# A decode block on one core: wo in contiguous blocks, the last K load ahead of the last V loads, the MLP weights in pieces

## The chip, the cores and the metric

The kernel runs on one core of a Trainium2 chip. The metric is the device time of one execution in microseconds (us). The profiled execution has a *span*, from its first to its last instruction; the timed number is about 1.8 us longer. Here a run counts as slow when it is over 1.5% above the fastest of its kernel.

## The reference

One token for each of four sequences goes through an attention block with a K/V cache and then an MLP. The shapes decide everything: the cache is 268 MB, the weights are 15 MB, the arithmetic is tiny.

```python
# x: (4,1,640) bf16; k_cache, v_cache: (4,32,4096,128); wq: (640,4096); wo: (4096,640)
# w1: (640,1728); b1: (1728); w2: (1728,640)
def A(x):                                     # attention
    q = (x @ wq).reshape(4, 1, 32, 128).transpose(0, 2, 1, 3)
    p = softmax(einsum("bhqd,bhkd->bhqk", q, k_cache) * 128 ** -0.5)
    return einsum("bhqk,bhkd->bhqd", p, v_cache).transpose(0, 2, 1, 3).reshape(4, 1, 4096) @ wo
def B(x):                                     # MLP with mish
    h = x @ w1 + b1
    return (h * tanh(softplus(h))) @ w2
h = x + A(layernorm(x))
return h + B(layernorm(h))
```

## The kernel before

The cache is read in 64 *tiles*. A tile is two heads of one sequence: 2,048 KB of K and 2,048 KB of V, each one load in which a partition takes one run of 16,384 bytes (64 positions of 128 numbers). I write K62 for the K load of tile 62; the last one is 63. All large loads come from one queue, in the order of the program, and the trace has 16 completions of each, which I take for one of each of the core's 16 DMA engines.

```python
LA = 3                                        # loads are issued three tiles ahead
stream = ctx.enter_context(tc.tile_pool(name="stream", bufs=8))     # 8 slots of 2 MB
def load_wo():                                # runs of 1,280 bytes, into three of the K/V slots
    for h0 in range(0, H, WOH):
        ...
        nc.sync.dma_start(
            out=v, in_=A_wo[h0 * Dh : (h0 + nh) * Dh, :].rearrange("(h p) n -> p h n", p=P))
...
WO_AT = NT - 4                                # wo is loaded ahead of tile 60, the MLP weights last
for i in range(NT + 1):
    if i + LA < NT:
        if i + LA == WO_AT:
            load_wo()
        load_kv(i + LA)                       # K, then V
    elif i + LA == NT:
        load_mlp()
    ...
```

Each tile passes through four steps. VectorE (DVE) multiplies K by q, in two halves (`prod`). TensorE (PE) sums the products with an identity as weights into PSUM (where the kernel keeps the sums of its matmuls), 256 columns at a time (`red`, called the fold below), DVE adds up what is left (`s_f`), ScalarE (ACT) takes exp (`e`). Then PE multiplies with V: 64 matmuls a tile, each with 128x128 of V as weights and two columns of e.

```python
def emit_pv(i):
    ...
    for r in range(R):                        # R = 64
        nc.tensor.matmul(o_ps[hg][:, b, :], lhsT=vt[i][:, r, :], rhs=e_bufs[i % NE][:, r, :],
                         start=(r == 0), stop=(r == R - 1))
```

After the last tile all products with wo follow in the tail (`y_ps`), then the layernorm and the MLP (`h_ps`, `act`, `y2_ps`).

The softmax here doesn't subtract the row's maximum and nothing guards it: scores larger than these inputs give would overflow.

## Time and profile before

| | before |
|---|---|
| time, median of 3 runs | 693.4 us |
| profiled span | 691.6 us |
| bytes moved | 283.4 MB |
| K62 landed | 650.6 us |
| K63 landed | 660.3 us |
| last load (end of w2) landed | 677.2 us |

From the page of the kernel before: the span; busy time, share of the span and number of instructions by engine; the rate in 40 slices of 17.3 us; packet sizes; one of the DMA queues; and the chain that ended last.

```profile
span 691.6 us, 14314 instructions
...
PE 486.5 (70%) x6663; PEld 383.4 (55%) x6663; DVE 338.4 (49%) x263; ACT 64.6 (9%) x288; POOL 1.6 (0%) x14
...
GB/s 373 428 424 428 431 422 425 430 425 428 425 428 427 425 426 429 425 424 431 425 425 427 427 426 427 424 429 426 424 427 430 424 427 426 417 337 427 420 373 18
DMA packets 25815, 284.28 MB, mean 411 GB/s; under 512 B 2260, under 2 KB 8092, under 8 KB 8732
...
q8 instruction: 52, 0.85, 0.5%
...
DMA 76%; PE 15%; DVE 7%; issue 1%; SPq 0%; DVEq 0%; ACT 0%
```

The stream runs at 424 to 430 GB/s nearly all the time; no compute engine is full. It is short of that in the first slice, in the slice around 610 us (337 GB/s) and in the last two. The line "q8 instruction" is the one that matters most later, and I passed over it: 52 packets, 0.85 MB, so 16 KB each, are fetches of instructions, and the page counts their time on the same 16 DMA engines as that of the data (0.5% of their span). PE has 6,663 matmuls and as many weight loads, so 13,326/52 = 256 instructions to a fetch; in the kernel after it is 11,792/46 = 256 and in e9 6,514/25 = 261.

The windows view of the kernel before (each line: start:end, length, busy time of the engines, then PE clock, DMA share and GB/s at the end) shows what the two weak places cost.

```profile
0.00:600.00 600.00, 430.39 (x5707) 336.90 (x5708) 304.71 (x222) 55.73 (x254) 1.56 (x14) 0.77 1.00 425
600.00:624.00 24.00, 14.25 (x200) 11.37 (x198) 7.59 (x5) 1.97 (x9) 0.00 (x0) 0.74 0.96 352
624.00:670.00 46.00, 29.27 (x405) 23.42 (x405) 20.89 (x15) 2.77 (x16) 0.00 (x0) 0.69 1.01 421
670.00:677.00 7.00, 5.40 (x190) 5.27 (x187) 0.71 (x2) 1.98 (x5) 0.00 (x0) 0.72 0.55 196
```

From 600 to 624 us the rate is 352 GB/s: at 427 this loses 24 x (1 - 352/427) = 4.2 us. There wo comes in small packets (1,280 bytes, 0.059 us each on average, 22 GB/s per engine; a packet of 16,384 bytes took 0.616 us, 26.6 GB/s), and its last part waits for a slot (4.7 us for PE's `o_ps` in the issue that stands from 610.16 to 615.47 us; the rate from 608 to 610 us is 224 GB/s). From 670 to 677 us the rate is below half.

The chain that ended last, from the kernel before (start, length, what). Its end:

```profile
646.33 14.02 DMA k_6961<-in_A_k_cache_dram
...
660.47 2.30 DVE prod L225
...
672.04 2.10 PE y_ps L297 x76
...
675.90 1.78 issue
...
678.45 0.42 PE y_ps L297 x10
...
680.14 2.09 PE h_ps L361 x70
```

K63 lands at 660.35, its multiply starts at 660.47, and the last product with wo is done at 678.87. From there to the end there are 12.7 us of layernorm and MLP, among them the 70 small matmuls of the first MLP product:

```profile
L361 PE MATMUL h_ps<-hb,w_sb x70: 166/167/215, 679.9 to 682.0; 128*128 128x5 bf16 x65, 128*64 128x5 bf16 x5
```

### The profile page before, as it was taken

The page shows a single profiled execution, that of the slowest core. Times are in us where ns is not written, and L with a number is a line of the kernel's source. Part 1 is how long each engine was busy: PE and PEld are TensorE (multiplying, and loading weights), DVE is VectorE, ACT ScalarE, POOL GpSimd, SP SyncE. Part 2 cuts the span into 40 slices and gives each one's busy share as a digit, 9 for nine tenths or more (in the row PEclk, how much of TensorE's full clock was granted, in tenths as well). Part 3 has the DMA queues.
Part 4 walks back from the last instruction along what each step waited for, and adds up shares of the span by engine and source line. Part 5 has one row for each costly group of instructions (what it writes and reads, how often), then busy time and mean ns, then how long its engine had stood idle before and what let it go on. Part 6 is the DMA issues. An engine that isn't in the chain of part 4 may idle for free.

```text
span 691.6 us, 14314 instructions
## 1 busy us (share of the span) xinstructions
PE 486.5 (70%) x6663; PEld 383.4 (55%) x6663; DVE 338.4 (49%) x263; ACT 64.6 (9%) x288; POOL 1.6 (0%) x14
## 2 busy tenths in 40 slices
PE   2976767766866687767768777667687657853875
PEld 0455556645655566556546655556566546632674
DVE  2535644554454646544654555355455644523532
ACT  1301000100001010100100010000001000000011
POOL 0000000000000000000000000000000000000000
PEclk9967787867678657789776688887768986765785
DMA  9999999999999999999999999999999999999990
GB/s 373 428 424 428 431 422 425 430 425 428 425 428 427 425 426 429 425 424 431 425 425 427 427 426 427 424 429 426 424 427 430 424 427 426 417 337 427 420 373 18
DMA packets 25815, 284.28 MB, mean 411 GB/s; under 512 B 2260, under 2 KB 8092, under 8 KB 8732
## 3 DMA queue, kind: packets, MB, share of 16 engines
q1 hardware_dynamic: 25720, 283.36, 97.2%
q8 instruction: 52, 0.85, 0.5%
q14 instruction: 7, 0.06, 0.0%
q10 hardware_dynamic: 36, 0.01, 0.0%
HBM read 283.35 MB, written 0.01 MB: 410 GB/s over the span
## 4 chain that ended last, share of the span: by engine, by line
DMA 76%; PE 15%; DVE 7%; issue 1%; SPq 0%; DVEq 0%; ACT 0%
PE red L238 9%; DVE prod L225 7%; DMA k_1410<-in_A_k_cache_dram 5%; DMA k_3784<-in_A_k_cache_dram 5%; DMA k_92<-in_A_k_cache_dram 5%; DMA k_1863<-in_A_k_cache_dram 5%; DMA k_4690<-in_A_k_cache_dram 5%; DMA k_5596<-in_A_k_cache_dram 5%; DMA k_3331<-in_A_k_cache_dram 5%; DMA k_2425<-in_A_k_cache_dram 5%; DMA k_6049<-in_A_k_cache_dram 5%; DMA k_4237<-in_A_k_cache_dram 5%; DMA k_2878<-in_A_k_cache_dram 5%; DMA k_957<-in_A_k_cache_dram 5%; DMA k_6502<-in_A_k_cache_dram 5%; DMA k_5143<-in_A_k_cache_dram 5%
## 5 line engine op out<-in xcount | busy, mean ns | idle before, releaser
L238 PE MATMUL red<-prod,ident 128*128 128x256 bf16 x2048 | 350.2, 345 | 182.7 <-DVE prod L225 182.7
L238 PEld LDWEIGHTS <-ident 128*128 128x128 bf16 x2048 | 243.2, 121 | 265.8 <-issue 172.0
L248 DVE TENSOR_REDUCE s_f<-red 128x64 f32<-128x512 f32 x64 | 43.8, 684 | 5.0 <-PE red L238 5.0
L268 DVE RECIPROCAL rl<-l_ps 128x8 f32<-128x8 f32 x16 | 3.3, 208 | 43.9 <-PE l_ps L260 43.9
L253 ACT ACTIVATE e_123<-s_f 64x64 bf16<-64x64 f32 x32 | 8.8, 274 | 159.2 <-DVE s_f L248 158.8
L253 ACT ACTIVATE e_119<-s_f 64x64 bf16<-64x64 f32 x32 | 8.8, 276 | 147.3 <-DVE s_f L248 147.0
L253 ACT ACTIVATE e_117<-s_f 64x64 bf16<-64x64 f32 x32 | 8.8, 275 | 137.1 <-DVE s_f L248 136.7
L215 ACT CAST qbc<-qb_ps 128x512 bf16<-128x512 f32 x16 | 9.4, 586 | 96.3 <-PE qb_ps L210 96.3
L225 DVE TENSOR_TENSOR prod<-k_6622,qbc 128x4096 bf16<-128x4096 bf16 x2 | 4.5, 2266 | 18.8 <-DMA k_6622<-in_A_k_cache_dram 18.8
L253 ACT ACTIVATE e_121<-s_f 64x64 bf16<-64x64 f32 x32 | 8.8, 276 | 44.0 <-DVE s_f L248 43.7
L197 PEld LDWEIGHTS <-lnT 128*4 128x4 bf16 x40 | 3.9, 102 | 15.6 <-issue 13.6
L225 DVE TENSOR_TENSOR prod<-k_84,qbc 128x4096 bf16<-128x4096 bf16 x2 | 4.5, 2288 | 13.5 <-DMA k_84<-in_A_k_cache_dram 13.5
L210 PE MATMUL qb_ps<-q_all,sel 4*128 4x128 bf16 x128 | 10.7, 228 | 0.0
L210 PEld LDWEIGHTS <-sel 4*128 4x128 bf16 x128 | 7.9, 99 | 5.1 <-issue 5.1
L197 PE MATMUL q_ps<-wq_76,lnT 128*4 128x512 bf16 x16 | 6.9, 508 | 3.8 <-DMA wq_76<-in_A_wq_dram 3.8
L197 PE MATMUL q_ps<-wq_73,lnT 128*4 128x512 bf16 x16 | 7.1, 529 | 0.7 <-DMA wq_73<-in_A_wq_dram 0.7
L225 DVE TENSOR_TENSOR prod<-k_4690,qbc 128x4096 bf16<-128x4096 bf16 x2 | 4.6, 2286 | 6.2 <-DMA k_4690<-in_A_k_cache_dram 6.2
L225 DVE TENSOR_TENSOR prod<-k_5940,qbc 128x4096 bf16<-128x4096 bf16 x2 | 4.6, 2286 | 6.1 <-DMA k_5940<-in_A_k_cache_dram 6.1
L225 DVE TENSOR_TENSOR prod<-k_2425,qbc 128x4096 bf16<-128x4096 bf16 x2 | 4.6, 2288 | 6.0 <-PE red L238 6.0
L225 DVE TENSOR_TENSOR prod<-k_92,qbc 128x4096 bf16<-128x4096 bf16 x2 | 4.6, 2286 | 6.1 <-DMA k_92<-in_A_k_cache_dram 6.1
L225 DVE TENSOR_TENSOR prod<-k_1180,qbc 128x4096 bf16<-128x4096 bf16 x2 | 4.5, 2266 | 6.1 <-DMA k_1180<-in_A_k_cache_dram 6.1
L225 DVE TENSOR_TENSOR prod<-k_88,qbc 128x4096 bf16<-128x4096 bf16 x2 | 4.6, 2288 | 5.3 <-PE red L238 5.3
(272 smaller groups left out, 579.3 us busy)
## 6 DMA issues: line engine op xcount, KB each, us to landing
w_sb<-in_B_w_dram SPq DMA_DIRECT2D x1, 2160.0 KB
w_sb<-in_B_w_dram SPq DMA_DIRECT2D x1, 2080.0 KB, 28.3
wq_73<-in_A_wq_dram SPq DMA_DIRECT2D x2, 1024.0 KB, 5.8
wq_76<-in_A_wq_dram SPq DMA_DIRECT2D x2, 1024.0 KB, 8.9
k_84<-in_A_k_cache_dram SPq DMA_DIRECT2D x1, 2048.0 KB
v_86<-in_A_v_cache_dram SPq DMA_DIRECT2D x1, 2048.0 KB, 19.8
k_88<-in_A_k_cache_dram SPq DMA_DIRECT2D x1, 2048.0 KB
v_90<-in_A_v_cache_dram SPq DMA_DIRECT2D x1, 2048.0 KB
```

What stands on the lines that cost most here:

```text
L197: nc.tensor.matmul(q_ps[:, :], lhsT=lnT[:, c, :], rhs=wq_t[c // 2][:, o : o + 512], start=(c == 0), stop=(c == DC - 1),)
L210: nc.tensor.matmul(q_ps[:, b, :], lhsT=sel[:, b, g, :], rhs=q_all[:, h * Dh : (h + 1) * Dh], start=(g == 0), stop=(g == G - 1),)
L215: nc.scalar.copy(out=t[:, :, :], in_=q_ps[:, :, :])
L225: nc.vector.tensor_tensor(out=t[:, :, :], in0=kt[i][:, s * RS : (s + 1) * RS, :], in1=q_bc[hg][:, b, :].unsqueeze(1).to_broadcast([P, RS, ...
L238: nc.tensor.matmul(reds[i][:, s * RS : (s + 1) * RS, :], lhsT=ident[:, :], rhs=t[:, :, c * CW : (c + 1) * CW], start=(c == 0), stop=(c == ...
L248: nc.vector.tensor_reduce(out=s_f[:, :], in_=reds.pop(i)[:, :, :], axis=AX.X, op=ALU.add)
L253: nc.scalar.activation(out=e_bufs[i % NE][sl, :, g], in_=s_f[sl, :], func=ACT.Exp, scale=SCALE, accum_out=rs_bufs[hg % 2][sl, b, g : g + 1],)
L268: nc.vector.reciprocal(out=rl[hg][:, :], in_=l_ps.pop(hg)[:, :])
```

## The change

Its intent is to remove the weak places: no small packets and no wait for a slot at wo, less work after the last K, larger packets for w2.

- wo is loaded in four contiguous blocks of 8 heads with runs of 10,240 bytes, into buffers of its own, each block when its heads are nearly done. The rows then lie in another order over the partitions, so 64 small matmuls permute the attention output of the block (`a_ps`), and three of the four products with wo leave the tail.
- K63 is loaded ahead of V62 and V63, V63 in two pieces.
- w1 and w2 come in two pieces each. w2 has 13 consecutive rows per partition, with runs of 7,680 to 8,960 bytes. The first MLP product must then take its columns with a step of 13, that is of 26 bytes. The last 64 rows of w2 come at the head.
- The fold takes 512 columns at a time, so half as many fold matmuls, and `s_f` and the product with V are taken in halves of a tile; there are seven slots, and loads are issued two tiles ahead.

```diff
+    CW = 512 // RS
 ...
+    NSLOT = 7
+    LA = 2
 ...
+    def load_wo(k):
+        t = consts.tile([P, WB, D], BF16, tag="wo", name=f"wo{k}")
+        nc.sync.dma_start(
+            out=t[:, :, :],
+            in_=A_wo[k * WB * Dh : (k + 1) * WB * Dh, :].rearrange("(p j) n -> p j n", j=WB),
+        )
 ...
+        w2_v = B_w2[0 : FM * P, :].rearrange("(p j) n -> p j n", j=FM)
+        for j0, j1 in zip(W2S, W2S[1:]):
+            nc.sync.dma_start(out=w2_sb[:, j0:j1, :], in_=w2_v[:, j0:j1, :])
 ...
+    loads.append((load_cache, kt, A_k_cache, NT - 1, "k"))
+    loads.append((load_cache, vt, A_v_cache, NT - 2, "v"))
+    loads.append((load_cache, vt, A_v_cache, NT - 1, "v", 2))
+    for k in reversed(range(H // WB)):
+        loads.insert(min(2 * ((k + 1) * TPB - 1), 2 * (NT - 2)), (load_wo, k))
 ...
+    def emit_wo(k):
+        a_ps = ps.tile([P, WB, N], FP32, tag="misc", name="a_ps")
+        for j in range(WB):
+            for h in range(WB):
+                nc.tensor.matmul(
+                    a_ps[:, j, :],
+                    lhsT=perm[:, j, PADW - h * QW : PADW - h * QW + P],
+                    rhs=OT[:, k * WB + h, :],
+                    start=(h == 0), stop=(h == WB - 1),
+                )
 ...
+                    w = w1_sb[:, c, 0 : FM * P].rearrange("p (f j) -> p j f", j=FM)[:, j, :]
```

## The prediction

> **What bounds the kernel.** The stream of K and V from HBM. Over 34 to 600 us the windows view gives 427 GB/s, PE 72% and DVE 52% busy; the chain of waits is 76% DMA. 283.4 MB at 427 GB/s is 664 us, so about 28 us of the 691.6 us span can be won. They lie in: the first 17 us (370 GB/s, 2.3 us lost); the load of wo at 600 to 624 us (352 GB/s, 4.2 us lost); the end of the stream, where the rate falls from 400 to 150-300 GB/s between 670 and 677 us (3 to 4 us lost); and about 14.5 us after the last byte (677 us).
>
> **What changes.**
> 1. wo comes in four blocks with 10,240-byte runs instead of 1,280, in its own buffer, so no K waits for slots held by wo. In the DMA records a 1,280-byte packet took 0.059 us (22 GB/s per engine), a 16,384-byte one 0.616 us (26.6). [...] The queue also ran dry (224 GB/s at 608-610 us): wo's last part waited for a slot. Gain 4 us.
> 2. w2 in runs of 7,680 and 8,960 bytes, its tail loaded at the head. Estimate: 2 us gained; engines finishing unevenly still cost 2 us.
> 3. Last K ahead of the last two V: 8.55 MB follow K63 instead of 6.5, so it lands another 4.9 us earlier, but 5 us after K62: DVE and PE then limit.
> 4. Three quarters of wo's products leave the tail; the last block adds 64 permuting matmuls (about 1.9 us), and a copy (0.5).
> 5. Folds of 512 columns, half as many matmuls: same PE time; two score reductions of 0.68 us per tile instead of one: DVE needs 6 of 9.8 us per tile, off the path. Seven slots leave about 14 us of loads queued instead of 18: enough.
>
> **Critical path.** Estimate: the last byte lands at 669 instead of 677, K62 at 644. With the trace's durations (multiply 2.28, fold 3.5 cold and 1.8 warm, 64 PV matmuls 1.75, reduction 0.69, exp 1.0): fold of K63 done 657.8, sum 660.3, both PV 664, wo finished 668. From the last wo matmul to the end the trace has 12.7 us, giving 681. I add 1 us for stalls like PE's 1.8 us "issue" gap at 676, and 1 us because the first MLP product now reads weights with a 26-byte step: [...] no run shows this yet. Total 683 of span; the timed runs are 1.8 us above the span: 684.5 us.
>
> **Prediction.** 684.5 us, 680 to 689 in 8 of 10 cases. Faster by over 2%: 0.12; within 2%: 0.85; slower by over 2%: 0.03.
>
> **What the profile would show.** No dip near 600 us, slices of 424 to 430 GB/s to the end; packets under 2 KB down from 8,092 to about 2,500; w2 landed before its product starts, so the tail is a chain of PE and DVE; 13 to 15 us from last byte to end; 70 matmuls of the first MLP product in 2.3 to 4 us (before 2.3).
>
> **What would make it wrong.** The queue running dry with seven slots; strided weights costing far over 1 us; uneven engines costing as much at the end as before.

668 for wo, 12.7 to the end, 1 for stalls and 1 for the strided weights make 683 of span, and with 1.8 more it was put at 684.5. The last 1 us was the author's guess, with nothing measured behind it; the kernel after shows 2.3 (4.6 against 2.3 us for the 70 matmuls). "Cold" and "warm" are granted clocks: in the kernel before the fold at 662.81 us took 3.54 us at 0.52 of the full clock, the one at 667.93 took 1.77 us at 1.00. "Same PE time" for the folds: 350.2 us busy before, 321.0 after.

## The result, and the profile after

The kernel after takes 690.0 us (median of 4 runs, 689.29 to 690.4), against 693.3 us for the kernel before in the same rounds. The ratio is 0.9955, with a 95% interval of 0.9938 to 0.9973: same, within 2%. A ratio is always the mean time of one kernel's fast runs over that of the other's fast runs of the same rounds, so it is not quite the ratio of the medians. The predicted direction and class hold, but 690.0 lies above the range of 680 to 689, and 5.5 us above the point.

The page of the kernel after, the same lines:

```profile
span 687.5 us, 12940 instructions
...
PE 465.7 (68%) x5896; PEld 266.8 (39%) x5896; DVE 382.6 (56%) x331; ACT 64.8 (9%) x288; POOL 3.0 (0%) x14
...
GB/s 357 433 429 426 426 424 428 427 427 425 426 428 427 428 427 426 425 426 427 428 427 426 425 426 430 429 425 426 423 427 428 428 427 425 426 427 427 428 353 32
DMA packets 21207, 284.20 MB, mean 413 GB/s; under 512 B 2520, under 2 KB 2592, under 8 KB 3360
...
q8 instruction: 46, 0.75, 0.4%
...
DMA 57%; PE 20%; DVE 19%; ACT 2%; issue 1%; SPq 0%; DVEq 0%; ACTq 0%
```

The dip at 610 us is gone, and so are the small packets, 8,092 down to 2,592, as predicted. The last two slices are not full, where 424 to 430 to the end were predicted, and the first is weaker than before (357 against 373).

The windows view of the kernel after:

```profile
0.00:600.00 600.00, 407.99 (x5008) 229.08 (x5009) 339.18 (x280) 55.02 (x250) 2.96 (x14) 0.81 1.00 425
600.00:624.00 24.00, 18.60 (x228) 10.43 (x228) 14.87 (x11) 2.79 (x13) 0.00 (x0) 0.86 1.01 430
624.00:664.00 40.00, 24.13 (x285) 13.12 (x281) 23.79 (x19) 3.06 (x18) 0.00 (x0) 0.83 1.00 422
664.00:675.00 11.00, 8.37 (x249) 7.96 (x250) 1.68 (x10) 1.69 (x4) 0.00 (x0) 0.60 0.47 192
```

From 600 to 624 us the rate is 430 instead of 352. But the stretch with less than half the rate, 7 us long before, is now 11 us long, and it loses 11 x (1 - 192/427) = 6.1 us instead of 7 x (1 - 196/427) = 3.8 us. So the new kernel's gain at wo comes with a longer end of its stream.

The chain that ended last, from the kernel after:

```profile
620.83 28.32 DMA k_6443<-in_A_k_cache_dram
...
649.24 2.30 DVE prod L251
...
655.87 2.28 DVE prod L251
...
664.87 3.33 PE o_ps L300 x128
...
668.44 1.70 PE a_ps L323 x58
...
670.87 1.13 issue
672.00 0.92 PE y_ps L334 x28
...
674.25 4.58 PE h_ps L400 x70
```

k_6443 is K62. From its landing on, DVE, PE and ACT work without a wait for data: 649.14 to 672.92 (last product with wo) is 23.8 us. The last piece of w2 lands at 674.5 and is needed only at 681.65. The first MLP product takes twice as long as before (200 against 167 ns as the records show each matmul, but 65 against 32 ns from one to the next):

```profile
L400 PE MATMUL h_ps<-hb,w_sb x70: 193/200/221, 674.2 to 678.6; 128*128 128x5 bf16 x65, 128*64 128x5 bf16 x5
```

The gain in span of 4.1 us, in three stretches of the two chains:

| | before | after | difference |
|---|---|---|---|
| start of K63's multiply | 660.47 | 655.87 | -4.6 |
| from there to the last wo product | 18.40 | 17.05 | -1.35 |
| from there to the end | 12.7 | 14.6 | +1.9 |

### K62: which engine is late

K62 heads the new chain, and the prediction had it at 644. In both kernels the same bytes come ahead of it (wq, 62 tiles, all of wo), but for the last 64 rows of w2 (0.08 MB) in the kernel after. The trace has the 16 completions of each large load, at different times, and what needs the load starts after the last: in the kernel after those of K62 run from 639.65 to 649.14 us, and DVE, idle for 5.47 us before, starts its multiply at 649.24 (for K63 in the kernel before 655.66 to 660.35, and 660.47). For K62, in us:

| K62's 16 completions | before | after | difference |
|---|---|---|---|
| first | 645.86 | 639.65 | -6.2 |
| mean of the 16 | 648.22 | 644.34 | -3.9 |
| last, when K62 can be used | 650.59 | 649.14 | -1.5 |

The mean gained 3.9 us, just what was predicted for wo, and stands at the predicted 644. But DVE waited for the last engine, and that one gained 1.5 us. The distance from the first to the last completion grew through the run in both kernels:

| at about (us) | 50 | 150 | 300 | 450 | 600 | 650 | 672 |
|---|---|---|---|---|---|---|---|
| before: last minus first (us) | 1.9 | 3.3 | 5.0 | 8.0 | 9.7 | 4.7 | 6.0 |
| before: instruction fetches so far | 2 | 9 | 21 | 33 | 44 | 47 | 49 |
| after: last minus first (us) | 1.8 | 2.4 | 4.9 | 6.9 | 8.4 | 9.5 | 9.9 |
| after: instruction fetches so far | 2 | 8 | 18 | 29 | 39 | 42 | 44 |

Three things are to be seen. The distance grows with the fetches. It falls from 9.7 to 4.7 us in the kernel before where the queue ran dry at wo (DMA share 0.54 and 224 GB/s from 608 to 610 us). I read this as the late engines catching up while those ahead had nothing to do. And the 16 engines fall into two groups of eight: at K62 of the kernel after, the eighth completion is 3.1 and the ninth 7.8 us behind the first.

### The profile page after: what moved, and what is told of

Its sections match the earlier page's. It is cut to its first block, busy times and chain, and to the rows that moved or that the text cites. A ratio compares the mean times of both kernels' runs of the same rounds, so it can differ in the third digit from the quotient of the medians.

```text
span 687.5 us, 12940 instructions
## 1 busy us (share of the span) xinstructions
PE 465.7 (68%) x5896; PEld 266.8 (39%) x5896; DVE 382.6 (56%) x331; ACT 64.8 (9%) x288; POOL 3.0 (0%) x14
## 2 busy tenths in 40 slices
DMA packets 21207, 284.20 MB, mean 413 GB/s; under 512 B 2520, under 2 KB 2592, under 8 KB 3360
## 4 chain that ended last, share of the span: by engine, by line
DMA 57%; PE 20%; DVE 19%; ACT 2%; issue 1%; SPq 0%; DVEq 0%; ACTq 0%
DVE prod L251 16%; PE red L263 11%; DMA k_6443<-in_A_k_cache_dram 4%; DMA k_1559<-in_A_k_cache_dram 4%; DMA k_3256<-in_A_k_cache_dram 4%; DMA k_4953<-in_A_k_cache_dram 4%; DMA k_366<-in_A_k_cache_dram 4%; DMA k_2857<-in_A_k_cache_dram 4%; PE o_ps L300 4%; DMA k_4157<-in_A_k_cache_dram 4%; DMA k_763<-in_A_k_cache_dram 3%; DMA k_1160<-in_A_k_cache_dram 3%; DMA k_4554<-in_A_k_cache_dram 3%; DMA k_6144<-in_A_k_cache_dram 3%; DMA k_2460<-in_A_k_cache_dram 3%; DMA k_5854<-in_A_k_cache_dram 3%
## 5 line engine op out<-in xcount | busy, mean ns | idle before, releaser
L263 PE MATMUL red<-prod,ident 128*128 128x512 bf16 x1024 | 321.0, 470 | 131.4 <-DVE prod L251 130.0
L263 PEld LDWEIGHTS <-ident 128*128 128x128 bf16 x1024 | 112.8, 115 | 275.0 <-issue 217.7
L272 DVE TENSOR_REDUCE s_f<-red 128x32 f32<-128x512 f32 x128 | 87.9, 687 | 44.5 <-PE red L263 44.5
L287 PE MATMUL l_ps<-rs_126,ones_f 128*128 128x8 f32 x16 | 4.7, 369 | 35.6 <-ACT e_124 L280 13.9
L306 DVE TENSOR_TENSOR OT<-o_ps,rl 128x8 bf16<-128x8 f32 x16 | 2.7, 167 | 43.9 <-PE o_ps L300 43.9
L287 PE MATMUL l_ps<-rs_128,ones_f 128*128 128x8 f32 x16 | 4.3, 344 | 30.3 <-ACT e_122 L280 11.6
L287 PEld LDWEIGHTS l_ps<-rs_126,ones_f 128*128 128x128 f32 x16 | 4.0, 310 | 36.3 <-ACT e_124 L280 14.2
L287 PEld LDWEIGHTS l_ps<-rs_128,ones_f 128*128 128x128 f32 x16 | 3.6, 280 | 31.4 <-ACT e_120 L280 11.0
L251 DVE TENSOR_TENSOR prod<-k_84,qbc 128x4096 bf16<-128x4096 bf16 x2 | 4.5, 2288 | 14.3 <-DMA k_84<-in_A_k_cache_dram 14.3
L223 PE MATMUL q_ps<-wq_77,lnT 128*4 128x512 bf16 x16 | 6.7, 497 | 4.6 <-DMA wq_77<-in_A_wq_dram 4.6
L251 DVE TENSOR_TENSOR prod<-k_1452,qbc 128x4096 bf16<-128x4096 bf16 x2 | 4.6, 2287 | 8.2 <-DMA k_1452<-in_A_k_cache_dram 8.2
L251 DVE TENSOR_TENSOR prod<-k_4846,qbc 128x4096 bf16<-128x4096 bf16 x2 | 4.6, 2288 | 7.2 <-DMA k_4846<-in_A_k_cache_dram 7.2
L280 ACT ACTIVATION_READ_ACCUMULATOR e_120<-s_f 64x1 f32 x44 | 8.1, 185 | 0.0
L251 DVE TENSOR_TENSOR prod<-k_3149,qbc 128x4096 bf16<-128x4096 bf16 x2 | 4.6, 2288 | 6.2 <-DMA k_3149<-in_A_k_cache_dram 6.2
```

What stands on the lines that cost most here:

```text
L223: nc.tensor.matmul(q_ps[:, :], lhsT=lnT[:, c, :], rhs=wq_t[c // WQC][:, o : o + 512], start=(c == 0), stop=(c == DC - 1),)
L251: nc.vector.tensor_tensor(out=t[:, :, :], in0=kt[i][:, s * RS : (s + 1) * RS, :], in1=q_bc[hg][:, b, :].unsqueeze(1).to_broadcast([P, RS, ...
L263: nc.tensor.matmul(red[:, :, :], lhsT=ident[:, :], rhs=t[:, :, c * CW : (c + 1) * CW], start=(c == 0), stop=(c == Dh // CW - 1),)
L272: nc.vector.tensor_reduce(out=s_t[i][:, s * RS : (s + 1) * RS], in_=reds.pop((i, s))[:, :, :], axis=AX.X, op=ALU.add,)
L280: nc.scalar.activation(out=e_bufs[i % NE][sl, :, g], in_=s_t[i][sl, :], func=ACT.Exp, scale=SCALE, accum_out=rs_bufs[hg % 2][sl, b, g : g ...
L287: nc.tensor.matmul(l_ps[hg][:, :], lhsT=ones_f[:, :], rhs=rs_bufs[hg % 2][:, :, :].rearrange("p b g -> p (b g)"), start=True, stop=True,)
```

## The experiments

**Theory.** Each fetch of 256 PE instructions holds up one of the same eight DMA engines by about 1.5 us. A load waits for the slowest engine, so this adds up. The stall at wo in the kernel before let the late engines catch up, so it cost less than its lost bytes, and taking it away gives back less. **Rivals.** The engines are late because of PE's work, not its instructions; and a stall in the queue costs just the bytes that it misses. Of the tail, the question is what each part of the change did: the order of K63, the blocks of wo, the rows of w2.

All experiments start from the kernel after, except where another is named. The ratio is to the kernel before.

### e1_half_pv: fewer instructions

Half of the V matmuls of tiles 0 to 55 are left out. The result is wrong (the comparison with the reference is too coarse to notice it).

```diff
-        for r in range(s * RS, (s + 1) * RS):
+        step = 2 if i < 56 else 1
+        for r in range(s * RS, (s + 1) * RS, step):
 ...
```

> The kernel after, with only every second PV product for the tiles below 56 (wrong result on purpose; loads, waits and the last eight tiles are as they were). This takes 1,792 matmuls and as many weight loads away, so about 14 of the 46 instruction fetches of 16 KB. Theory (each fetch holds up one and the same eight DMA engines by about 1.5 us, and every load lands with its slowest engine): spread of the 16 engines' landings at the end 9.9 -> 7.3 us, K62 lands 2.6 us earlier (649.2 -> 646.6), time about 2.6 us shorter. Rival (the engines drift apart for a reason in the data stream itself): spread stays at 9.9, K62 at 649, time within 0.5 us.

Measured: 32 fetches instead of 46. First to last completion 6.8 us instead of 9.9 at the end, K62 at 646.8 instead of 649.1. The time was 686.8 us, ratio 0.9912 [0.9899, 0.9926]. The same bytes land earlier when PE has fewer instructions. By itself this doesn't separate the fetches from PE's work.

### e2_fold256: more instructions, the same work

The folds take 256 columns again, as before the change: twice as many fold matmuls of half the size, and so the same sum on PE.

```diff
-    CW = 512 // RS
+    CW = 256 // RS
```

> The kernel after, with folds of 256 columns as before: 1,024 more matmuls with their weight loads, the same columns in all, result right. About 8 more instruction fetches (46 -> 54). Theory: spread at the end 9.9 -> 11.4 us, K62 lands 1.5 us later, time 1 to 1.5 us longer. Rival (drift from the data stream): no change of spread or of K62's landing, time within 0.5 us.

Measured: 54 fetches, first to last 11.4 us at K62 (9.5 in the kernel after) and 11.6 at the end, K62 at 651.3 (+2.2), ratio 0.9972 [0.9958, 0.9985] against 0.9955. The landing moved by 0.7 us more than the theory's 1.5; most of this was there from the start, as the mean completion at 26 us is 0.6 us later in this run. The time moved by 0.17%, and these two intervals overlap a little. Together, and with e9 below, the effect is proportional to the fetches. At K62, mean of the late eight completions minus mean of the early eight:

| | e9 | e1 | after | e2 |
|---|---|---|---|---|
| fetches until K62 | 21 | 28 | 42 | 50 |
| late eight minus early eight (us) | 3.5 | 4.5 | 7.5 | 9.0 |

Between the two ends, (9.03 - 3.49) / ((50 - 21) / 8) = 1.5 us per fetch on the engine that it falls on. A fetch itself is 0.9 to 1.1 us (mean 1.06 in both kernels), a data packet of that size 0.616. Why it costs more than its own time is not shown here.

The trace of the kernel after also shows this fetch by fetch, when the 16 completions of each load are compared with those of the load before. From 30 to 668 us there are 43 fetches, and 43 times one engine falls back by 1.4 to 1.7 us against the others, each time around a fetch (in e2 it is 51 and 51). At 662 us five of the late engines are 7.8 to 8.3 us behind the first and three are 9.4 to 10.0 us behind. This is five and six steps of about 1.55 us, and 5 x 5 + 3 x 6 = 43, as if the fetches went round these eight. The early eight have steps of their own, eight of 0.6 to 1.0 us, each around one of eight smaller instruction packets (8 KB, queue q14). So I put the 3.1 us of the eighth completion down to instruction packets as well, but to these, and e2 has as many of them (eight).

### e4_drain: a stall put in

In the load queue, ahead of K60, a tiny copy waits for V59. The queue runs dry, as before the change, but with no small packets.

```diff
+    def drain(i):
+        nc.sync.dma_start(out=sc[:, :], in_=vt[i][0:N, 0, 0:2])
 ...
+    loads.insert(at[0], (drain, 59))
```

> The kernel after, with a stall put in: a tiny copy ahead of K60 makes the queue wait until V59 has landed on all engines. Theory: the leading engines lose up to 9 us[...], so K62 lands about 2 us later, the spread after it is under 2 us instead of 9.5, and the time grows by 2 us at most (or even less, since V63, w1 and w2 land together), although the dip holds 5 to 7 us worth of bytes. Rival (a dip costs what it holds): K62 and the end come 5 to 7 us later.

Windows of this run:

```profile
604.00:608.00 4.00, 1.58 (x42) 1.39 (x40) 2.26 (x2) 0.58 (x1) 0.00 (x0) 1.00 1.01 426
608.00:612.00 4.00, 3.92 (x29) 1.71 (x29) 3.08 (x4) 0.82 (x4) 0.00 (x0) 0.57 0.96 406
612.00:616.00 4.00, 2.96 (x57) 1.94 (x55) 0.93 (x2) 0.00 (x0) 0.00 (x0) 1.00 0.57 240
616.00:620.00 4.00, 2.14 (x7) 0.81 (x7) 4.00 (x3) 0.69 (x4) 0.00 (x0) 0.79 0.41 176
```

From 600 to 624 us the rate was 303 instead of 430 GB/s, which is 24 x (1 - 303/430) = 7.1 us worth of bytes. The mean completion of K62 came 6.7 us later (651.0 instead of 644.3), but its last only 3.4 us later (652.6). First to last fell from 8.3 to 1.9 us. The ratio is 0.9998 [0.9986, 1.0011], 0.43% or 3.0 us more than the kernel after. So this stall cost about half of its bytes, with the engines apart: the cost of 3 us misses the theory's 2 by 1, and the rival's 5 to 7 by more. This is the catching up of the kernel before, made on purpose.

### e3_w2_chunks: w2 by rows of 128 again

w2 and b1 in the order of before (b1 transposed on PE at the head, not shown), so that the first MLP product reads its weights without a step. The two pieces stay.

```diff
-        w2_v = B_w2[0 : FM * P, :].rearrange("(p j) n -> p j n", j=FM)
+        w2_v = B_w2[0 : FM * P, :].rearrange("(j p) n -> p j n", p=P)
-                    w = w1_sb[:, c, 0 : FM * P].rearrange("p (f j) -> p j f", j=FM)[:, j, :]
+                    w = w1_sb[:, c, j * P : (j + 1) * P]
```

> The kernel after, with w2, w1 and b1 read in the layout of before (w2 in 1,280-byte rows, weights of the first MLP product contiguous). Theory: the 70 matmuls of the first MLP product go from 4.6 back to about 2.3 us and all of it is on the chain, so 2.3 us shorter; w2's end comes about 1 us later and is not waited for. Rival (w2 lands too late with short rows): the last product waits for w2 and the gain is under 1 us.

The 70 matmuls of the first MLP product in this run:

```profile
L406 PE MATMUL h_ps<-hb,w_sb x70: 166/167/216, 674.1 to 676.4; 128*128 128x5 bf16 x65, 128*64 128x5 bf16 x5
```

They take 2.4 us, nearly the 2.3 of before the change, instead of 4.6. K62 and the last piece of w2 land as in the kernel after (649.1 and 674.6), although w2's packets are small again. The ratio is 0.9916 [0.9902, 0.9929], 0.39% or 2.7 us better. So 13 rows per partition are a loss: w2 lands 7 us ahead of its use (674.5 against 681.65 in the kernel after), and larger packets there bought nothing.

### e11_k_order: K63 after V62 again

```diff
-    loads.append((load_cache, kt, A_k_cache, NT - 1, "k"))
     loads.append((load_cache, vt, A_v_cache, NT - 2, "v"))
+    loads.append((load_cache, kt, A_k_cache, NT - 1, "k"))
```

> The kernel after with the order of the last loads of before (V62 ahead of K63). Theory: K63 lands at about 659 instead of 654, the second tile's multiply starts at about 659.1 instead of 655.9, and the end comes 3 us later: about 693 us, so that this order is worth about as much as the whole change brought. Rival: under 1 us later, as PE is the limit there.

K63's multiply starts at 659.4 instead of 655.9; the ratio is 0.9986 [0.9974, 0.9999]. The order of K63 is worth 0.31%, 2.1 us, about two thirds of what the whole change gained. I expected 3 us. The multiply comes 3.5 us later, but the tail behind it is 0.8 us shorter here (30.8 us from that start to the end, 31.6 in the kernel after): PE's "issue" gap ahead of the last wo products is 0.31 us in this run instead of 1.13.

### e12_wo_rows: the blocks of wo by rows again

wo in runs of 1,280 bytes, still four blocks at four times in buffers of their own; no permuting.

```diff
-            in_=A_wo[k * WB * Dh : (k + 1) * WB * Dh, :].rearrange("(p j) n -> p j n", j=WB),
+            in_=A_wo[k * WB * Dh : (k + 1) * WB * Dh, :].rearrange("(h p) n -> p h n", p=P),
 ...                                            # the 64 permuting matmuls and the copy are gone
-                    y_ps[:, c, :], lhsT=t[:, j, c * P : (c + 1) * P], rhs=a[:, j, :],
+                    y_ps[:, c, :], lhsT=t[:, h, c * P : (c + 1) * P], rhs=OT[:, k * WB + h, :],
```

> The kernel after with wo still in four blocks, but in the 1,280-byte rows of before and without the permuting matmuls and their copy. Theory: the four loads take about 2.6 us more in all (5.24 MB at 22 instead of 26.6 GB/s per engine), K62 lands at about 651.5, and the tail is 2.5 us shorter without the permutation: the time stays within 0.7 us. Rival (the long runs are worth more than the permutation costs): 2 us or more slower.

K62 lands at 651.45 (+2.3), and the ratio is 0.9961 [0.9949, 0.9974] against 0.9955: the same. The small packets cost what their records say: 4,096 of them at 0.059 us, against 0.048 us for 1,280 bytes at 26.6 GB/s, over 16 engines, is an estimate of 2.8 us. But the last block's permuting matmuls and the copy stand on the chain with about 2 us (1.70 and 0.20 in the chain above), so the larger packets as such gained nothing. (In this run PE also stood 1.87 us in an "issue" gap in the tail, 1.13 in the kernel after, so the version without permuting may be a little better than this run.)

### e5_wo_late: e3, and the last block of wo behind K62 and K63

```diff
-        loads.insert(min(2 * ((k + 1) * TPB - 1), 2 * (NT - 2)), (load_wo, k))
+        loads.insert(2 * ((k + 1) * TPB - 1) if k < 3 else 2 * (NT - 2) + 2, (load_wo, k))
```

> The kernel of the w2-chunks run, with the last wo block (1.31 MB, 3.1 us of stream) loaded after K62 and K63 instead of ahead of them. Theory (the tail is a chain from K62's landing): K62 lands at about 646 instead of 649.1, the end comes 3 us earlier, about 684 us timed; w2 lands at 674 as before. Rival (the tail is bound by the last bytes): no gain beyond 0.5 us.

K62's multiply starts at 646.1, 3 us earlier, and the time is 683.35 us, ratio 0.9861 [0.9849, 0.9874], 0.55% or 3.8 us better than e3. So the tail does hang on K62, whatever is loaded after it.

### e6_k_first: e5, and K62 and K63 also ahead of V61

The last block of wo comes behind V63 here, and PE takes the V matmuls of the last three tiles after all folds.

```diff
+        NT - 2: [(load_cache, kt, A_k_cache, NT - 2, "k"), (load_cache, kt, A_k_cache, NT - 1, "k"),
+                 (load_cache, vt, A_v_cache, NT - 3, "v")],
+        NT - 1: [(load_cache, vt, A_v_cache, NT - 2, "v"), (load_cache, vt, A_v_cache, NT - 1, "v", 2),
+                 (load_wo, H // WB - 1), (load_mlp,)],
```

> The run before, and K62 and K63 also ahead of V61 (PV of the last three tiles after all folds). Theory: K62 lands at about 641 and the chain from it no longer binds; then the last bytes do: w2 lands at 674 and the last product, the output and the store take about 7 us more, about 682.5 us timed. If the chain still bound, it would be about 679; if PE is held up by the late V61, no gain over the run before (684).

A miss: 685.2 us, ratio 0.9889 [0.9874, 0.9903], slower than e5. K62 landed at 640.9, another 5 us earlier, but then DVE and PE were not done with tile 61: in the chain the last wait for data ends at 626 us, and PE lost 2.0 and 1.7 us in "issue" gaps. The earlier data gained nothing here, as the work on it was the limit.

### e7_w2_six: e6, and the last piece of w2 on fewer engines

The second piece of w2 is split in partitions 0 to 113 and 114 to 127. I meant the larger one to go to six engines only, and its six completions below show that it did. Which six was not shown. A clause on this is cut from the expectation: "those" in it are the engines of the larger piece.

```diff
+        for p0, p1 in ((0, 114), (114, P)):
+            nc.sync.dma_start(out=w2_sb[p0:p1, 7:FM, :], in_=w2_v[p0:p1, 7:FM, :])
```

> The run before, with the second piece of w2 split by rows into 114 and 14[...]. If those are among the eight that are ahead: the late ones are spared about 2.5 us, w2 lands at about 671.5 and the time falls by 2 to 2.5 us. If they are among the late ones: w2 lands at about 678 and the time grows by about 4 us. If the lag is not of certain engines: w2 later by a few us too.

The time was 688.5 us, ratio 0.9932 [0.992, 0.9944], 0.43% or 3.3 us by the medians over e6. The large piece does have six completions: four at 674.8 us, one at 676.8 and the last at 681.8. The small piece landed at 682.1 instead of e6's 674.4 for the whole, and PE's last product waited 1.8 us for it. So a load was not kept off the late engines this way. One late engine among the six fits these times (an estimate: its 114 packets of 0.059 us take 6.7 us, so it began at about 675.1, when the last engines finished w2's first piece, 674.6 to 675.8). But the traces don't number the engines, so which are late stays open. Nor is the wait all of the loss, as PE's two "issue" gaps in the tail are 1.7 us longer together than in e6.

### e8_pv_wide: e6, with fewer and larger V matmuls

e becomes the weights (8 columns) and V the moving side (512 columns): 16 matmuls a tile instead of 64. They form all products of four positions with four, of which a mask keeps the diagonal, and four small matmuls sum it.

```diff
+                nc.tensor.matmul(
+                    w_ps[i][:, :, :],
+                    lhsT=e_bufs[i % NE][:, r : r + RB, :].rearrange("p r g -> p (r g)"),
+                    rhs=vt[i][:, r : r + RB, :],
+                    start=(r == 0), stop=(r == R - RB),
+                )
 ...
+                nc.vector.tensor_tensor(
+                    out=wm[:, :, :], in0=w_ps.pop(i)[:, :, :], in1=dmask[:, :, :], op=ALU.mult
+                )
```

> The K-first run, with the PV product of tiles 0 to 59 as 16 matmuls of 512 columns (the eight exp columns stationary) and a masked sum instead of 64 matmuls of 2 columns; result right. PE does 1.7 us more per tile at full clock, but 5,280 instructions go, about 20 of 46 fetches. Theory: spread at the end 9.7 -> 6 us, w2 lands 3.5 us earlier, about 679 us timed although PE works more. Rival (fetches don't matter; PE's work does): the same time as the K-first run or slower.

(The 1.7 us are an estimate from the trace of the kernel after: at a clock of 1.00 a fold of 4,096 columns took 1.75 us at 70.02 us, so 8,192 columns take 3.5, and the 64 V matmuls that go took 1.75.)

A failure: 816 us, ratio 1.177 [1.173, 1.181]. One line of its waits view (who waited for whom: us, times, longest) and one of its windows tell why:

```profile
DVE wm L335 <- PE pvw L327: 294.4, 60, 5.9
...
100.00:500.00 400.00, 304.56 (x1440) 112.39 (x1440) 205.08 (x178) 26.85 (x136) 0.00 (x0) 0.86 0.93 352
```

The mask stands in DVE's order ahead of the next multiply of K, and waits 294.4/60 = 4.9 us in each tile for PE. So the slots come free late, and the stream runs at 352 GB/s. This run says nothing against the theory; it is an error of order.

### e9_pv_wide2: e5, with the wide V matmuls and the mask one step later

The same matmuls in e5, but DVE masks the tile before the last, which PE has long done.

```diff
+            if s == 0 and i - 2 in w_ps:
+                emit_wm(i - 2)
 ...
+            if s == 0 and i - 2 in wms:
+                emit_wsum(i - 2)
```

> The wo-late run with the wide PV product for tiles 0 to 59, its masked sum now taken one step later, so that the multiply of the next K no longer waits for it (in the first wide run it did, 4.7 us per tile). Theory: PE needs about 8 us of the 9.8 us per tile, the stream stays fed, about 20 of 46 fetches are gone, spread at the end about 6 us, K62 lands at about 642.5 instead of 646, about 680 us timed. Rival (PE or a wait of PE is now slower than the stream): again far slower than 693 us, with dips of DMA through the whole run.

The page of this run:

```profile
span 679.0 us, 7722 instructions
...
PE 559.5 (82%) x3257; PEld 224.2 (33%) x3257; DVE 419.5 (62%) x396; ACT 64.8 (10%) x288; POOL 3.3 (0%) x14
...
GB/s 367 422 427 431 425 425 430 428 422 430 427 424 429 424 425 431 423 429 428 427 427 423 428 429 421 430 428 427 424 431 424 425 428 430 421 430 425 426 415 159
...
q8 instruction: 25, 0.41, 0.2%
```

680.8 us, ratio 0.9823 [0.981, 0.9837]: the best version, 1.8% faster than the kernel before, and correct. PE is *busier* than in any other version that keeps up with the stream (559.5 us, 8.7 a tile, against 465.7) and has the fewest instructions, and the stream ends the fullest. This takes away the rival that PE's work makes the engines late: first to last is 5.3 us with 25 fetches. The chain now hangs on V63:

```profile
637.40 23.33 DMA v<-in_A_v_cache_dram
...
660.77 1.03 PE o_ps L331 x32
```

### e10_k_halves: e5, K62 and K63 in two halves each

```diff
-    loads.append((load_cache, kt, A_k_cache, NT - 1, "k"))
+    loads.append((load_cache, kt, A_k_cache, NT - 1, "k", 2))
 ...                                            # the same for K62
```

> The wo-late run with K62 and K63 each loaded in two pieces, so that the first multiply of K62 can start when half of it has landed. Theory (chain of DVE and PE from K62's landing): first half at about 643.7 instead of 646.1, the end 2 us earlier, about 681.3 us timed; w2 at 674.4 then begins to bind. Rival (PE and DVE work on the last two tiles is what binds, or PE starts colder): under 0.7 us gained.

683.0 us, ratio 0.9855 [0.984, 0.987] against e5's 0.9861: nothing to speak of. The landing of V63, at about 664, takes over the chain as soon as K's multiply starts earlier.

## Why the prediction was right or wrong

- **Right: the bound, and the class.** The stream bounds both kernels, the dip at wo is gone, the small packets fell to 2,592 (about 2,500 predicted), and faster within 2% is what came.
- **Wrong, and the step that failed: "the last byte lands at 669 instead of 677, K62 at 644".** Measured are 674.5 and 649.1. The term mis-sized is "engines finishing unevenly still cost 2 us". For the last piece of w2 the mean of the 16 completions is 669.5 and the last 674.5; for K62 they are 644.3 and 649.1. Its two times are met by the average engine within half a microsecond, but the last engine is 5 us behind that. This closeness is partly luck: the prediction doesn't say how it came to 669, but 664 for the bytes, 2.3 for the head and 2 for the uneven engines make 668, so the 2 us were probably in it already. Counted in bytes, the last 11 us of the stream lose 6.1 us.
- **With it failed "Gain 4 us" for wo.** The average gained 3.9 us, K62 1.5. In the kernel before the stall had let the late engines catch up (9.7 to 4.7 us), and in the kernel after nothing does. e4 made such a stall: 7 us of bytes, 3 us of time. The gain was there, and was given back at the end of the stream.
- **It could have been seen.** The kernel before had K62 at 650.6 in its trace. With the same bytes ahead and 4 us gained it could at best come at 646.6; I never set 644 against that. The spread of the completions was in that trace as well (4.7 us for K62, 6.0 for the end of w2). The prediction named the risk ("uneven engines costing as much at the end as before") and gave it no size.
- **The cause of the lag is the fetches.** The lag goes with their number over four kernels (1.5 us each on one of eight engines), down with fewer instructions (e1, e9), up with more of the same work (e2), and not with PE's busy time (e9); and in the kernel after each of the 43 steps of the late engines stands at a fetch. What is not shown is why a fetch costs more than its own 1 us, and why only eight engines are hit.
- **Right: the chain from K62 on.** Predicted were 24 us from K62 to the last wo product (644 to 668), measured 23.8; after that 15 (12.7 and two allowances), measured 14.6. In these the strided weights were allowed 1 us, a guess, and cost 2.3 (2.3 to 4 us were named for the product, 4.6 measured), and of the 1 us for stalls PE's "issue" gap took 1.13, ahead of the last wo product. That the sum still fits is partly luck: the last product took 2.1 us instead of 2.9. The gap is probably a fetch too: on the chains of all these runs PE has 14 "issue" gaps of 0.3 to 2.0 us after 640 us, each ends 1.2 to 1.5 us after the packet of a fetch, and where a run has two, they are 256 PE instructions apart. No run tested this.
- **Wrong: "Estimate: 2 us gained" for w2.** The mean completion of the last load did come earlier, but w2 is not on the chain, and its order costs 2.3 us of the first MLP product (e3: 2.7 us better without it).
- **Smaller, and not tested by a run:** the head is 0.6 to 0.9 us later in the kernel after (0 to 17 us: 358 against 370 GB/s), perhaps because the loads of b1 in its new order (runs of 26 bytes) and of w2's tail now share the first stretch with wq. The order of b1 is not the main part: with the old one the first multiply of K starts at 21.0 us in e3, against 21.4 in the kernel after and 20.5 in the kernel before.

The sum: 5.1 us of the miss are K62's landing; the rest of the chain came out 0.6 us shorter than predicted (23.8 + 14.6 = 38.4 against 39). That gives 4.5 us in the span (687.5 against 683). The profiled run was the fastest of four and the median lies 0.7 us higher. The remaining 0.3 of the 5.5 us is a slip of the prediction: 683 and 1.8 are 684.8, not 684.5.

## What to carry to other kernels

In a kernel bound by its loads, look at the completions of the single DMA engines and not only at the rate: here a load was used when its slowest engine was done (K62: mean 644.3, last 649.1, multiply at 649.24), and a lag that had built up through the run (1.8 us at 50 us, 9.9 at 672) was paid at the end, where no later load hid it (6.1 us of bytes). PE's instructions were a part of the DMA load as well (a fetch for each 256, about 1.5 us on one of the late engines), so fewer and larger matmuls were faster even where PE had time to spare (e9, 680.8 us against 683.35 in e5). And a stall in the middle of the stream cost less than its missing bytes (3.0 against 7.1 us in e4), so removing one can gain less.
